# Whole float32 operands for the product of probabilities and values in the first of four batches

## The chip, the cores and the metric

The kernel runs on one core of a Trainium2 chip. The metric is the device time of one execution in microseconds (us). A core has five engines that work side by side, each through its own list of instructions in order: PE (TensorE, matrix products), DVE (VectorE), ACT (ScalarE), POOL (GpSimd) and SP (SyncE, which here only issues DMA transfers). PEld is PE's loading of the stationary operand, which can overlap a running product. An engine waits for another through semaphores.

## The reference

```python
def _attn_ref(q, k, v, tau):                       # q, k, v: (4, 8, 576, 64), float32
    scores = scale * np.matmul(q, k.transpose(0, 1, 3, 2))
    thresh = np.max(scores, axis=-1, keepdims=True) - tau
    scores = np.where(scores >= thresh, scores, -1000000000.0)
    scores = scores - np.max(scores, axis=-1, keepdims=True)
    attn = np.exp(scores)
    attn = attn / (np.sum(attn, axis=-1, keepdims=True) + 1e-09)
    return np.matmul(attn, v).astype(np.float32)
...
x = _moe_ref(x, w_in, w_out, alpha)    # h = x @ w_in (512 -> 2048); leaky max; @ w_out (2048 -> 512)
return _moe2_ref(x, w_in, w_out)       # h = x @ w_in; h * clip(h + 3, 0, 6) / 6; @ w_out
```

x has 2304 rows: 4 batches of 576 positions, 8 heads of 64 columns. The weights of both feed-forward networks (FFNs) come as float64 and are decoded to float32 on the chip.

## The kernel before

**Split operands.** Products run on operands of type float32r (`F32R`), which hold only the upper part of a float32. To keep the precision, a float32 operand is split: ACT copies it to float32r (`hi`), and another engine subtracts that from the source (`lo`). A product is then three: hi by hi, lo by hi, hi by lo.

**Attention.** The work goes through 16 pairs of heads (4 in each batch) and 9 tiles of 128 query rows in each pair, so a batch has 36 tiles. For tile `i` the stages are: `do_S` (scores, PE, into the PSUM tile `s`, of which there are 2), `soft_max` (DVE, maximum), `soft_exp` (ACT), `soft_keep` (DVE, threshold and sum), `soft_den` and `soft_rc` (POOL and DVE, reciprocal; POOL then scales the row `e`, L403, and copies its last 64 columns once more, L404), `do_T` (PE transposes four blocks of `e` as float32, L429), then the split of the transposed probabilities into `pt`, and once every two or three tiles a unit is complete: `do_R` transposes the last 64 columns (L448, split at L450 and L451), `do_PV` multiplies probabilities and values (PE, L465), and `do_x` adds the two halves of the result into `xo` (ACT L479, DVE L484). A pair has 4 units: two of 256 columns (buffer `ptu`) and two of 320 (buffer `ptw`).

**The product before.** The stationary operand `vn` is 128 wide: 64 columns of the upper parts of the values beside 64 of the lower ones. It meets 4 blocks of upper parts of the probabilities, one block in which the last 64 keys have upper over lower parts, and 4 blocks of lower parts, so a unit takes 9 products. The lower parts of the transposed probabilities come from DVE (L438), except that in the first two batches three tiles of nine (1, 4 and 7, `PE_LO`) take them from PE: a product with the negated identity `nidentr` (L435) subtracts the upper part in PSUM, and ACT copies the rest out (L436). The values are loaded by SP into a `raw` tile and split by ACT (L107) and POOL (L108; DVE for the first pair).

**FFNs.** From the end of the first batch on, the FFNs of batch b run in groups between the attention tiles of batch b + 1, after a fixed number of groups for each tile (`per`, with a lag of 3 tiles). Their first pass needs the decode of 64 weight chunks: ACT L136 and L137, DVE L138, L140 and L141, POOL L142, then a split. Six chunks are decoded early, during the first batch. The last batch's FFNs run alone at the end.

**Order.** The order of instructions on each engine is fixed when the program is built, by a scheduler that takes the code's order and priorities. At run time each engine keeps that order.

Of the kernel before, what the change touches and what calls it, by code (L numbers as in the profile page):

```python
# [9 lines left out]
F32 = mybir.dt.float32  # L10
F32R = mybir.dt.float32r
# [3 lines left out]
ALU = mybir.AluOpType  # L15
# [4 lines left out]
P = 128  # L20
NKT = 4
# The upper 32 bits of a float64, read as a float32: the least and greatest magnitude
# that float32's normal range holds.
# [9 lines left out]
def kernel(  # L33
# [13 lines left out]
    nc = tc.nc  # L47
    B, H, S, D = q.shape
# [4 lines left out]
    SM = 512  # L53
# [7 lines left out]
    # Weights decoded before the first FFN, and tiles by which the FFNs trail the attention.  # L61
    EARLY = 6
    LAG = 3
    # Tiles of a pair, up to tile PE_LO_END, whose lower parts come from the tensor engine.
    PE_LO = (1, 4, 7)
    PE_LO_END = 2 * PB
    # Chunks to a sum of the output.
# [4 lines left out]
    # Columns of a batch: 128 j + p holds position 4 p + j of the first 512; the other 64  # L72
    # positions of all batches make a block of their own.
# [22 lines left out]
    nidentr = const.tile([P, P], F32R, name="nidentr")  # L96
    nc.vector.tensor_single_scalar(nidentr, ident, -1.0, op=ALU.mult)
# [65 lines left out]
    # The FFNs in their order, each with the chunks of its weights; block None is the last  # L163
    # batch together with the last positions of all.
# [78 lines left out]
    # ------------------------------------------------------------------  # L243
    # attention, with the FFNs of the batches before it
    # ------------------------------------------------------------------
# [9 lines left out]
    # Queries of the two heads' last positions share a tile: each head's are beside zeros.  # L255
# [11 lines left out]
    # A pair of heads: of the first 512 positions, 4 to a partition, a block for each of the 4;  # L267
    # the last 64 of the one head are above those of the other, in block 4 between.
    def prep_load(pi, nm):
        if pi >= len(pairs):  # L270
            return
        b, hp = pairs[pi]
        src = {"q": q, "k": k, "v": v}[nm][b, 2 * hp:2 * hp + 2]
        t = a3.tile([P, 2, NB + 1, D], F32, tag="raw", name="raw")
        nc.sync.dma_start(t[:, :, 0:NB, :].rearrange("p h j d -> p h (j d)"),
                          src[:, 0:SM].rearrange("h (p j) d -> p h (j d)", j=NB))
        if nm == "v":
            for a in range(2):
                nc.sync.dma_start(t[64 * a:64 * a + 64, :, NB, :], src[:, SM:S].rearrange("h r d -> r h d"))
        else:  # L280
            for h in range(2):
                nc.sync.dma_start(t[64 * h:64 * h + 64, 0, NB, :], src[h, SM:S])
        st.setdefault(pi, {})["raw" + nm] = t.rearrange("p h j d -> p (h j) d")

    def prep_split(pi, nm):
        raw = st[pi].pop("raw" + nm)
        n = 2 * NB + 1
        if nm == "v":
            n += 1
            t = a2.tile([P, n, 2, D], F32R, tag="vn", name="vn")  # L290
        elif pi == 0 and nm == "q":
            t = a2.tile([P, 2 * NB + 2, 2, D], F32R, tag="vn", name="natq")
        else:
            t = a1.tile([P, n, 2, D], F32R, tag="nat", name="nat")
        raw = raw[:, 0:n]
        split(t[:, 0:n, 0, :], t[:, 0:n, 1, :], raw, nc.vector if pi == 0 else nc.gpsimd)
        st[pi]["nat" + nm] = t

    # Blocks 0 to 3 and 4 are the first head's columns; the second's begin with block 5, and
    # its last 64 come once more after block 8.  # L300
# [97 lines left out]
    # The last 64 probabilities of a row twice.  # L398
    def soft_rc(i):
        rc = small("rc", 3)  # L400
        nc.vector.reciprocal(rc, st.pop((i, "d")))  # L401
        e = st[i, "e"]
        nc.gpsimd.tensor_scalar(out=e[:, 0:S], in0=e[:, 0:S], scalar1=rc, scalar2=0.0, op0=ALU.mult, op1=ALU.add)  # L403
        nc.gpsimd.tensor_scalar(out=e[:, S:W], in0=e[:, SM:S], scalar1=1.0, scalar2=0.0, op0=ALU.mult, op1=ALU.add)  # L404

    # Where the transposed probabilities of a tile go: buffer, first column, and the unit
    # (head, first column, columns) that the tile completes.
# [8 lines left out]
    def pt_buf(i):  # L416
        nm = PLACE[i % NT][0]
        if i % NT in (0, 2, 7):
            ptb[nm] = a1.tile([P, 2 * NB + 1, {"u": 256, "w": 384}[nm]], F32R, tag="pt" + nm, name="pt" + nm,
                              bufs=2 if nm == "u" else 1)  # L420
        return ptb[nm]

    # Blocks 0 to 3: the upper parts of 128 keys each. Block 4: the upper parts of the last 64
    # over their lower parts. Blocks 5 to 8: the lower parts of 128 keys each.
    def do_T(i):
# [8 lines left out]
        if i < PE_LO_END and i % NT in PE_LO:  # L434
            nc.tensor.matmul(ps, lhsT=nidentr, rhs=pt[:, 0:NB], start=False, stop=True, skip_group_check=True)  # L435
            nc.scalar.copy(pt[:, NB + 1:], ps)  # L436
        else:
            nc.vector.tensor_tensor(out=pt[:, NB + 1:], in0=ps, in1=f32(pt[:, 0:NB]), op=ALU.subtract)  # L438

    def do_R(i):  # L440
# [5 lines left out]
        for j in range(m):  # L446
            e = st.pop((i - m + 1 + j, "e"))
            nc.tensor.transpose(ps[:, P * j:P * j + P], e[:, SM:W], ident)  # L448
        pt = ptb[nm][:, NB, c0 - (m - 1) * P:c0 + P]
        nc.scalar.copy(pt, ps)  # L450
        nc.vector.tensor_tensor(out=pt[64:P], in0=ps[64:P], in1=f32(pt[64:P]), op=ALU.subtract)  # L451

    def do_PV(i):
# [8 lines left out]
        pv = ps_ho.tile([P, SM], F32, tag="ho", name="pv")  # L462
        for kt in range(2 * NB + 1):
# [5 lines left out]
    def do_x(i):  # L469
# [8 lines left out]
        tl = a1.tile([P, 320], F32, tag="tl", name="tl")[hs]  # L478
        nc.scalar.copy(tl[:, 0:n], pv[ls, 0:n])  # L479
# [4 lines left out]
        nc.vector.tensor_tensor(out=xo[hs, d0:d0 + n], in0=pv[hs, 0:n], in1=tl[:, 0:n], op=ALU.add)  # L484
# [9 lines left out]
    # A group is 12 products of 512 columns: one chunk of 128 hidden features, or a quarter of  # L494
    # the output's sums over 4 chunks.
# [67 lines left out]
    # Rows of the output that a tile of 128 columns holds.  # L563
# [8 lines left out]
    # Weights that are decoded while there is no FFN yet.  # L572
# [18 lines left out]
    # No score reaches its row's maximum less a negative tau, and a row without any is  # L591
    # uniform: as if all scores were 0. So the scale of the queries is 0 then.
# [46 lines left out]
    # ------------------------------------------------------------------  # L639
    # both FFNs of the last batch together with the last positions  # L640
    # ------------------------------------------------------------------
# [84 lines left out]
```

## Time and profile before

| What | Value |
|---|---|
| Time, median of 3 runs (lowest to highest) | 1221.58 us (1220.2 to 1222.34) |
| Span of the profiled execution, first to last instruction | 1219.0 us |
| What lies around the span (median less span) | 2.6 us |
| PE, busy share of the span | 92% |
| DVE | 67% |
| POOL | 63% |
| ACT | 57% |
| Mean granted TensorE clock | 0.982 of full |

The profile is of one execution; its span lies 2.6 us under the median of the timed runs, and 1.2 us under the fastest. The shares are means over stages that differ much: the first 12 us are loads, up to 137 us only attention of the first batch and early decoding run, from 137 to 459 us FFNs of the first batch with all remaining decoding, then attention and FFNs without decoding, and from about 890 us FFNs alone. PE's busy time counts products whose ends are modelled, so it is above the time in which columns stream.

### The profile page before, as it was taken

The numbers are of one execution on the slowest core, as the hardware profiler recorded it, in microseconds if no ns is written. First come the engines' busy times: TensorE is split into PE (matmuls) and PEld (weight loads), VectorE is DVE, ScalarE is ACT, GpSimd is POOL, SyncE is SP. The second block draws the span as 40 slices with busy tenths as digits, with TensorE's granted clock in tenths as the row PEclk, the third lists the DMA queues.
The fourth block names the chain that finished last, engine by engine and source line by source line (L and its number), as shares of the span: only waits on it lengthen the run. The fifth ranks groups of instructions, "written<-read, shape, count | busy, mean of one in ns | idle before, by whom it ended". The sixth has DMA issues, their size and how long they took to land.

```text
span 1219.0 us, 18146 instructions
## 1 busy us (share of the span) xinstructions
PE 1124.4 (92%) x6008; PEld 949.6 (78%) x6008; DVE 814.9 (67%) x1607; ACT 699.7 (57%) x1280; POOL 770.5 (63%) x917
## 2 busy tenths in 40 slices
PE   5778988987788899999999999999999999999997
PEld 4667776875576688888888888887878888888886
DVE  7999997999899967687657576777645333332221
ACT  7888865766777765555665656455644222243432
POOL 4787798889779886766556776665533443434332
PEclk9889998999989999999999999999999999999999
DMA  6732345565557453424242444232224422222211
GB/s 196 227 115 74 97 142 170 157 184 167 184 154 219 141 163 105 120 80 113 77 121 79 131 137 121 70 96 74 71 78 129 118 60 68 61 61 63 67 35 52
DMA packets 95678, 139.51 MB, mean 114 GB/s; under 512 B 21472, under 2 KB 50656, under 8 KB 95584
## 3 DMA queue, kind: packets, MB, share of 16 engines
q1 hardware_dynamic: 95584, 138.36, 38.9%
q8 instruction: 47, 0.77, 0.3%
q14 instruction: 47, 0.39, 0.1%
HBM read 103.82 MB, written 25.17 MB: 106 GB/s over the span
## 4 chain that ended last, share of the span: by engine, by line
PE 56%; DVE 4%; issue 2%; POOL 2%; ACT 1%; DMA 1%; SPq 0%; POOLq 0%; DVEq 0%; ACTq 0%
PE h L204 24%; PE o L240 11%; PE o L234 9%; PE pv L465 3%; PE s L360 3%; PE t L429 2%; PE r L234 2%; PE r L240 2%; POOL wo L108 1%; DMA st<-wo 1%; PE pt L306 1%; DVE e L389 0%; PE r L448 0%; DVE wo L108 0%; DVE g L212 0%
## 5 line engine op out<-in xcount | busy, mean ns | idle before, releaser
L204 PE MATMUL h<-x,wi 128*128 128x512 f32 (+1 forms) x1536 | 360.2, 385 | 15.9 <-DVE g L212 4.8
L204 PEld LDWEIGHTS h<-x,wi 128*128 128x128 f32 x1536 | 275.0, 190 | 74.5 <-DVE g L212 5.5
L230 POOL TENSOR_TENSOR gs<-g,gs 128x512 fp32r<-128x512 f32 (+1 forms) x160 | 194.9, 1219 | 154.6 <-ACT gs L226 149.1
L240 PE MATMUL o<-wo,gs 128*128 128x512 f32 x768 | 195.8, 396 | 5.7 <-DVE g L220 1.8
L234 PE MATMUL o<-gs,wo 128*128 128x512 f32 x768 | 195.9, 397 | 1.3 <-POOL gs L230 0.8
L240 PEld LDWEIGHTS o<-wo,gs 128*128 128x128 f32 x768 | 141.0, 188 | 36.4 <-DVE g L220 2.9
L234 PEld LDWEIGHTS o<-gs,wo 128*128 128x128 f32 x768 | 141.2, 189 | 29.6 <-POOL gs L230 1.0
L226 ACT CAST gs<-g 128x512 fp32r<-128x512 f32 (+1 forms) x160 | 92.9, 580 | 87.3 <-DVE g L212 46.2
L220 DVE SCALAR_TENSOR_TENSOR g<-m,h 128x512 f32<-128x512 f32 x80 | 50.5, 631 | 132.4 <-ACT m L218 131.9
L403 POOL TENSOR_SCALAR e<-e,rc 128x576 f32<-128x576 f32 x144 | 115.1, 804 | 20.0 <-DVE rc L401 13.9
L389 DVE SCALAR_TENSOR_TENSOR e<-s,thr,e 128x576 f32<-128x576 f32 x144 | 116.0, 813 | 9.4 <-ACT e L382 7.5
L372 DVE TENSOR_REDUCE nmx<-s 128x1 f32<-128x576 f32 x144 | 107.1, 748 | 17.0 <-PE s L360 15.5
L382 ACT ACTIVATE e<-s,nmx 128x576 f32<-128x576 f32 x144 | 106.4, 748 | 19.4 <-DVE nmx L372 11.2
L209 DVE TENSOR_SCALAR m<-h,alpha_sb 128x512 f32<-128x512 f32 x80 | 55.3, 692 | 91.9 <-PE h L204 91.9
L360 PE MATMUL s<-ka,qt 128*128 128x288 f32 x512 | 103.5, 324 | 12.7 <-DVE e L389 11.5
L107 ACT CAST wo<-st 128x512 fp32r<-128x512 f32 x99 | 59.2, 620 | 91.4 <-DMA st<-wo 81.7
L218 ACT ACTIVATE m<-h,three 128x512 f32<-128x512 f32 x80 | 51.6, 646 | 102.9 <-PE h L204 102.6
L108 POOL TENSOR_TENSOR wo<-st,wo 128x512 fp32r<-128x512 f32 x58 | 76.0, 1324 | 51.8 <-ACT wo L107 51.8
L108 POOL TENSOR_TENSOR wi<-st,wi 128x512 fp32r<-128x512 f32 x58 | 74.8, 1291 | 45.7 <-ACT wi L107 44.9
L107 ACT CAST wi<-st 128x512 fp32r<-128x512 f32 x99 | 61.2, 619 | 66.2 <-PE h L204 27.9
L429 PE MATMUL t<-ident,e 128*128 128x128 f32 x576 | 91.4, 283 | 7.9 <-ACT ptu L436 3.0
L142 POOL TENSOR_TENSOR f<-f,low 128x512 uint32<-128x512 uint32 x64 | 86.3, 1348 | 19.5 <-issue 4.0
(103 smaller groups left out, 1942.7 us busy)
## 6 DMA issues: line engine op xcount, KB each, us to landing
st<-wi SPq DMA_DIRECT2D x99, 256.0 KB, 2.6
st<-wo SPq DMA_DIRECT2D x99, 256.0 KB, 2.6
raw<-in_moe_w_in_dram SPq DMA_DIRECT2D x32, 512.0 KB, 4.1
raw<-in_moe_w_out_dram SPq DMA_DIRECT2D x32, 512.0 KB, 3.9
ka<-ka SPq DMA_DIRECT2D x30, 304.0 KB, 4.2
wi<-f SPq DMA_DIRECT2D x32, 256.0 KB, 3.1
wo<-f SPq DMA_DIRECT2D x32, 256.0 KB, 4.1
raw<-in_k_dram SPq DMA_DIRECT2D x16, 256.0 KB, 2.9
```

The source lines that it names most:

```text
L107: nc.scalar.copy(hi, src)
L108: lo_eng.tensor_tensor(out=lo, in0=src, in1=f32(hi), op=ALU.subtract)
L204: nc.tensor.matmul(h[:, :n], lhsT=w[:, ws, kt * P:(kt + 1) * P], rhs=x[:, xs, kt, :n], start=(i == 0), stop=(i == len(steps) - 1))
L230: nc.gpsimd.tensor_tensor(out=gs[:, 1, :n], in0=g[:, :n], in1=f32(gs[:, 0, :n]), op=ALU.subtract)
L234: nc.tensor.matmul(o[:, :n], lhsT=w[:, ws, dt * P:(dt + 1) * P], rhs=gs[:, gsel, :n], start=fresh and start and i == 0, stop=stop and i == ...
L240: nc.tensor.matmul(o[:m, :], lhsT=gs[:, gsel, tt * P:tt * P + m], rhs=w[:, ws, :], start=start and i == 0, stop=stop and i == 2)
L360: nc.tensor.matmul(ps[:, half, 0:SH], lhsT=w, rhs=s["k"][:, a, h * W + half * SH:h * W + half * SH + SH], start=(n == 0), stop=(n == len(m ...
L372: nc.vector.tensor_reduce(out=nmx, in_=st[i, "s"][:, :, 0:SH], axis=AX.XY, op=ALU.max, negate=True)
L382: nc.scalar.activation(v2(e[:, 0:S]), st[i, "s"][:, :, 0:SH], AF.Exp, bias=st.pop((i, "nmx")), scale=1.0)
L389: nc.vector.scalar_tensor_tensor(out=v2(e), in0=st.pop((i, "s"))[:, :, 0:SH], scalar=st.pop((i, "thr")), in1=v2(e), op0=ALU.is_ge, op1=ALU ...
L403: nc.gpsimd.tensor_scalar(out=e[:, 0:S], in0=e[:, 0:S], scalar1=rc, scalar2=0.0, op0=ALU.mult, op1=ALU.add)
L429: nc.tensor.matmul(ps[:, j], lhsT=e[:, P * j:P * j + P], rhs=ident, is_transpose=True, start=(j == 0), stop=True, skip_group_check=True)
```

## The change

In batch 0 (`WHOLE = 1`) nothing of the product is split. The values are loaded straight into a tile of the pool and tag that the split values had (`a2`, tag `vn`, two buffers), and stay float32. The transposed probabilities are copied once from PSUM, as float32; the lower parts (L438) and the subtraction at L451 go, and so do the copy of the last 64 columns (L404) and the split of the values. A unit takes 5 products with both operands float32, and its result has 64 rows instead of 128, so `do_x` copies it once with ACT instead of copying one half and adding the other.

The route over the negated identity (`PE_LO`) is taken out altogether. In batch 0 nothing replaces it; in batch 1, where 12 tiles had used it, those tiles' lower parts now come from DVE, as in the later batches.

```diff
-    # Tiles of a pair, up to tile PE_LO_END, whose lower parts come from the tensor engine.
-    PE_LO = (1, 4, 7)
-    PE_LO_END = 2 * PB
+    WHOLE = 1
...
-    nidentr = const.tile([P, P], F32R, name="nidentr")
-    nc.vector.tensor_single_scalar(nidentr, ident, -1.0, op=ALU.mult)
...
     def prep_load(pi, nm):
...
+        whole = nm == "v" and b < WHOLE
+        if whole:
+            t = a2.tile([P, 2, 2, NB + 1, D], F32, tag="vn", name="vw")[:, 0]
+        else:
+            t = a3.tile([P, 2, NB + 1, D], F32, tag="raw", name="raw")
...
     def prep_split(pi, nm):
         raw = st[pi].pop("raw" + nm)
+        if nm == "v" and pairs[pi][0] < WHOLE:
+            st[pi]["natv"] = raw
+            return
...
     def soft_rc(i):
...
-        nc.gpsimd.tensor_scalar(out=e[:, S:W], in0=e[:, SM:S], scalar1=1.0, scalar2=0.0, op0=ALU.mult, op1=ALU.add)
+        if i >= WHOLE * PB:
+            nc.gpsimd.tensor_scalar(out=e[:, S:W], in0=e[:, SM:S], scalar1=1.0, scalar2=0.0, op0=ALU.mult, op1=ALU.add)
...
     def do_T(i):
...
         nc.scalar.copy(pt[:, 0:NB], ps)
-        if i < PE_LO_END and i % NT in PE_LO:
-            nc.tensor.matmul(ps, lhsT=nidentr, rhs=pt[:, 0:NB], start=False, stop=True, skip_group_check=True)
-            nc.scalar.copy(pt[:, NB + 1:], ps)
-        else:
+        if i >= WHOLE * PB:
             nc.vector.tensor_tensor(out=pt[:, NB + 1:], in0=ps, in1=f32(pt[:, 0:NB]), op=ALU.subtract)
...
     def do_R(i):
...
-            nc.tensor.transpose(ps[:, P * j:P * j + P], e[:, SM:W], ident)
+            if i < WHOLE * PB:
+                nc.tensor.transpose(ps[0:64, P * j:P * j + P], e[:, SM:S], ident)
+            else:
+                nc.tensor.transpose(ps[:, P * j:P * j + P], e[:, SM:W], ident)
         pt = ptb[nm][:, NB, c0 - (m - 1) * P:c0 + P]
+        if i < WHOLE * PB:
+            nc.scalar.copy(pt[0:64], ps[0:64])
+            return
...
     def do_PV(i):
...
+        if b < WHOLE:
+            for kt in range(NB + 1):
+                r = P if kt < NB else 64
+                nc.tensor.matmul(pv[0:64, 0:n], lhsT=vn[0:r, (NB + 1) * h + kt], rhs=src[0:r, kt, c0:c0 + n],
+                                 start=(kt == 0), stop=(kt == NB))
+            st[i, "v"] = pv
+            return
...
     def do_x(i):
...
+        if b < WHOLE:
+            nc.scalar.copy(xo[hs, d0:d0 + n], pv[0:64, 0:n])
+        else:
+            tl = a1.tile([P, 320], F32, tag="tl", name="tl")[hs]
+            nc.scalar.copy(tl[:, 0:n], pv[ls, 0:n])
+            nc.vector.tensor_tensor(out=xo[hs, d0:d0 + n], in0=pv[hs, 0:n], in1=tl[:, 0:n], op=ALU.add)
```

The scheduler places the instructions anew. PE's list before, at the third to fifth tile of the first pair, that is the unit of buffer `ptw` (`s` are scores, `t` and `r` transposes, `pt` the preparation of the next pair, `pv` the product):

```order
L448 MATMUL r<-ident,e 128x128 x3
L435 MATMUL t<-ptw,nidentr 128x512
L465 MATMUL pv<-ptw,vn 128x320 x4
L306 MATMUL pt<-identr,nat 128x128 x3
L360 MATMUL s<-ka,qt 128x288 x4
L429 MATMUL t<-ident,e 128x128 x4
L360 MATMUL s<-ka,qt 128x288 x4
L306 MATMUL pt<-identr,nat 128x128 x3
L465 MATMUL pv<-ptw,vn 128x320 x5
```

The same unit in the changed program, whose lines 366, 437, 454, 312 and 477 are the lines 360, 429, 448, 306 and 465 of before:

```order
L454 MATMUL r<-ident,e 64x128 x3
L312 MATMUL pt<-identr,nat 128x128 x3
L477 MATMUL pv<-ptw,vw 64x320 x5
L437 MATMUL t<-ident,e 128x128 x4
L366 MATMUL s<-ka,qt 128x288 x4
```

The nine products, which stood in two pieces with scores and transposes between them, have become five that stand together, and the product with `nidentr` is gone.

DVE's list before, in the second batch beside the first FFN groups, from the fourth tile of its first pair to the end of its `ptw` unit (`ptw<-t` is a lower part, L438; `m` and `g` belong to the FFN, `low` and `f` to the decoding):

```order
L438 TENSOR_TENSOR ptw<-t,ptw 128x4x128
L377 TENSOR_SCALAR thr<-nmx,ntau_sb 128x1
L389 SCALAR_TENSOR_TENSOR e,sm<-s,thr,e 128x576
L140 TENSOR_SCALAR f<-f 128x512
L209 TENSOR_SCALAR m<-h,alpha_sb 128x512
L141 TENSOR_SCALAR f<-f 128x512
L372 TENSOR_REDUCE nmx<-s 128x1
L212 SCALAR_TENSOR_TENSOR g<-h,m 128x512
L389 SCALAR_TENSOR_TENSOR e,sm<-s,thr,e 128x576
L401 RECIPROCAL rc<-den 128x1
L377 TENSOR_SCALAR thr<-nmx,ntau_sb 128x1
L451 TENSOR_TENSOR ptw<-r,ptw 64x384
```

The same place in the changed program (L443 is the lower part, L462 the subtraction of L451):

```order
L443 TENSOR_TENSOR ptw<-t,ptw 128x4x128
L383 TENSOR_SCALAR thr<-nmx,ntau_sb 128x1
L378 TENSOR_REDUCE nmx<-s 128x1
L443 TENSOR_TENSOR ptw<-t,ptw 128x4x128
L137 TENSOR_SCALAR f<-f 128x512
L135 TENSOR_SCALAR low<-raw_2166 128x512
L383 TENSOR_SCALAR thr<-nmx,ntau_sb 128x1
L407 RECIPROCAL rc<-den 128x1
L138 TENSOR_SCALAR f<-f 128x512
L395 SCALAR_TENSOR_TENSOR e,sm<-s,thr,e 128x576 x2
L206 TENSOR_SCALAR m<-h,alpha_sb 128x512
L462 TENSOR_TENSOR ptw<-r,ptw 64x384
```

A second lower part has come in, that of the fifth tile, which PE and ACT made before. In both programs 10 decodes stand ahead of the first FFN activation on DVE, and all 64 ahead of the 17th.

## Rows read from the trace of the kernel before

**Rows 1.** Busy time of each engine by stage; x counts instructions; PEclk is granted clock.

```profile
core 0: us, PE busy (x) PEld busy (x) DVE busy (x) ACT busy (x) POOL busy (x), PEclk, DMA share, GB/s
0.00:12.00 12.00, 4.95 (x26) 4.33 (x27) 4.34 (x14) 6.92 (x13) 0.70 (x6) 1.00 0.47 105
12.00:80.00 68.00, 48.48 (x268) 42.09 (x267) 63.50 (x153) 55.66 (x102) 54.24 (x80) 0.85 0.70 214
80.00:137.00 57.00, 48.93 (x342) 42.03 (x343) 53.76 (x140) 49.08 (x95) 38.59 (x78) 1.00 0.25 67
137.00:459.00 322.00, 275.92 (x1413) 225.69 (x1412) 287.37 (x522) 226.31 (x404) 278.83 (x299) 0.97 0.55 167
459.00:1219.00 760.00, 746.10 (x3965) 635.41 (x3963) 405.97 (x782) 361.70 (x669) 398.13 (x457) 1.00 0.31 87
```

**Rows 2.** PE's timeline about the first FFN product: start, length, line, count.

```profile
136.98 0.64 PE L465 MATMUL pv<-ptu,vn 128*128 128x256 f32 x4
137.46 2.66 PE L204 MATMUL h<-x,wi 128*128 128x512 f32 x11
```

**Rows 3.** DVE's groups of instructions, 12 to 137 us: busy, mean ns, idle before.

```profile
L389 DVE SCALAR_TENSOR_TENSOR e<-s,thr,e 128x576 f32<-128x576 f32 x40 | 32.2, 812 | 3.0 <-ACT e L382 2.3
...
L438 DVE TENSOR_TENSOR ptw<-t,ptw 128x512 fp32r<-128x512 f32 x16 | 10.7, 676 | 0.7 <-PE pv L465 0.7
L138 DVE TENSOR_SCALAR low<-raw 128x512 uint16<-128x512 uint16 x12 | 8.8, 735 | 0.2
...
L484 DVE TENSOR_TENSOR xo<-pv,tl 64x256 f32<-64x256 f32 (+1 forms) x16 | 7.2, 450 | 0.8 <-ACT tl L479 0.5
...
L451 DVE TENSOR_TENSOR ptw<-r,ptw 64x384 fp32r<-64x384 f32 (+1 forms) x8 | 4.0, 494 | 0.2
L451 DVE TENSOR_TENSOR ptu<-r,ptu 64x256 fp32r<-64x256 f32 x8 | 3.4, 428 | 0.2
...
L108 DVE TENSOR_TENSOR vn<-raw,vn 128x640 fp32r<-128x640 f32 x1 | 0.8, 826 | 2.0 <-ACT vn L107 2.0
```

**Rows 4.** ACT's and POOL's groups that the change touches, 12 to 137 us.

```profile
L436 ACT CAST ptu<-t 128x512 fp32r<-128x512 f32 x8 | 4.7, 585 | 0.0
L107 ACT CAST vn<-raw 128x640 fp32r<-128x640 f32 x5 | 3.6, 727 | 0.6 <-DMA raw<-in_v_dram 0.5
...
L436 ACT CAST ptw<-t 128x512 fp32r<-128x512 f32 x4 | 2.4, 598 | 0.0
L404 POOL TENSOR_SCALAR e<-e 128x64 f32<-128x64 f32 x38 | 10.6, 285 | 1.0
L108 POOL TENSOR_TENSOR vn<-raw,vn 128x640 fp32r<-128x640 f32 x5 | 7.8, 1552 | 0.0
```

**Rows 5.** PE's timeline, 100 to 110 us, all at full granted clock.

```profile
100.56 0.90 PE L465 MATMUL pv<-ptw,vn 128*128 128x320 f32 x5
101.29 0.60 PE L429 MATMUL t<-ident,e 128*128 128x128 f32 x4
101.65 0.77 PE L360 MATMUL s<-ka,qt 128*128 128x288 f32 x4
102.25 0.38 PE L306 MATMUL pt<-identr,nat 128*128 128x128 f32 x3
102.47 0.40 PE L448 MATMUL r<-ident,e 128*128 128x128 f32 x2
102.79 0.82 PE L465 MATMUL pv<-ptw,vn 128*128 128x320 f32 x4
...
105.55 0.63 PE L429 MATMUL t<-ident,e 128*128 128x128 f32 x4
105.94 0.99 PE L465 MATMUL pv<-ptw,vn 128*128 128x320 f32 x5
106.76 0.39 PE L435 MATMUL t<-ptu,nidentr 128*128 128x512 f32 x1
106.99 0.69 PE L360 MATMUL s<-ka,qt 128*128 128x288 f32 x4
107.52 0.63 PE L465 MATMUL pv<-ptu,vn 128*128 128x256 f32 x4
107.99 0.38 PE L448 MATMUL r<-ident,e 128*128 128x128 f32 x2
```

**Rows 6.** PEld's timeline, same place: weight loads of float32 transposes.

```profile
101.15 0.50 PEld L429 LDWEIGHTS t<-ident,e 128*128 128x128 f32 x4
101.62 0.56 PEld L360 LDWEIGHTS s<-ka,qt 128*128 128x128 f32 x4
```

**Rows 7.** DVE's groups, 137 to 459 us.

```profile
L138 DVE TENSOR_SCALAR low<-raw 128x512 uint16<-128x512 uint16 x52 | 47.6, 916 | 0.2
...
L438 DVE TENSOR_TENSOR ptw<-t,ptw 128x512 fp32r<-128x512 f32 x19 | 12.8, 680 | 4.9 <-ACT ptw L433 4.9
```

**Rows 8.** DVE's group L138, 80 to 130 us, one decode.

```profile
L138 DVE TENSOR_SCALAR low<-raw 128x512 uint16<-128x512 uint16 x1 | 0.5, 460 | 0.0
```

**Rows 9.** PE's timeline: the last use of the buffer `natq`.

```profile
11.51 0.54 PE L306 MATMUL pt<-identr,natq 128*128 128x128 f32 x3
```

**Rows 10.** SP's timeline of DMA issues: second pair's values, first weight chunk.

```profile
12.66 0.37 SPq L275 DMA_DIRECT2D raw<-in_v_dram  x1
...
16.20 0.59 SPq L130 DMA_DIRECT2D raw<-in_moe_w_in_dram  x1
```

More of the change, by code (lines that the diff above doesn't have):

```diff
@@ L273, in prep_load @@
         src = {"q": q, "k": k, "v": v}[nm][b, 2 * hp:2 * hp + 2]
-        t = a3.tile([P, 2, NB + 1, D], F32, tag="raw", name="raw")
+        whole = nm == "v" and b < WHOLE
[3 more added lines that the diff above has]
+            t = a3.tile([P, 2, NB + 1, D], F32, tag="raw", name="raw")
         nc.sync.dma_start(t[:, :, 0:NB, :].rearrange("p h j d -> p h (j d)"),
                           src[:, 0:SM].rearrange("h (p j) d -> p h (j d)", j=NB))
-        if nm == "v":
+        if whole:
+            nc.sync.dma_start(t[0:64, :, NB, :], src[:, SM:S].rearrange("h r d -> r h d"))
+        elif nm == "v":
             for a in range(2):
@@ L418, in pt_buf @@
         if i % NT in (0, 2, 7):
-            ptb[nm] = a1.tile([P, 2 * NB + 1, {"u": 256, "w": 384}[nm]], F32R, tag="pt" + nm, name="pt" + nm,
-                              bufs=2 if nm == "u" else 1)
+            ptb[nm] = a1.tile([P, 2 * NB + 1, {"u": 256, "w": 384}[nm]], F32 if i < WHOLE * PB else F32R, tag="pt" + nm,
+                              name="pt" + nm, bufs=2 if nm == "u" else 1)
         return ptb[nm]
@@ L477, in do_x @@
         hs, ls = slice(64 * h, 64 * h + 64), slice(64 - 64 * h, 128 - 64 * h)
-        tl = a1.tile([P, 320], F32, tag="tl", name="tl")[hs]
-        nc.scalar.copy(tl[:, 0:n], pv[ls, 0:n])
         if "xo" not in st[pi]:
@@ L483, in do_x @@
         d0 = 0 if nm == "u" else 256
-        nc.vector.tensor_tensor(out=xo[hs, d0:d0 + n], in0=pv[hs, 0:n], in1=tl[:, 0:n], op=ALU.add)
+        if b < WHOLE:
[4 more added lines that the diff above has]
+            nc.vector.tensor_tensor(out=xo[hs, d0:d0 + n], in0=pv[hs, 0:n], in1=tl[:, 0:n], op=ALU.add)
         if t == NT - 1:
```

## The prediction

> **What bounds the kernel now.** I read the busy times by stage first [rows 1], since the change touches only the first two batches. From 12 to 137 us, where batch 0's attention runs, DVE is busy 63.50 + 53.76 = 117.3 of 125 us, 94%. ACT has 104.7 (84%), POOL 92.8 (74%). PE's 97.4 counts modelled ends, so I work out its streaming below. DVE bounds this stage, and the stage ends where PE starts the first FFN product at 137.46 us [rows 2]. From 137 to 459 us DVE is busy 287.37 of 322 us (89%) and POOL 278.83 (87%), because all remaining decodes run there. After 459 us PE is busy 746 of 760 us: whatever is won or lost before is carried to the end, since PE has next to no idle time in which it could disappear.
>
> **What leaves DVE in batch 0.** Of 36 tiles, 24 have their lower part on DVE: 24 x 0.68 = 16.3 us. The 16 units lose the subtraction of L451 (8 x 0.494 + 8 x 0.428 = 7.4) and the addition of L484 (16 x 0.450 = 7.2), and the first pair's split of values goes (0.8) [rows 3]. Together 31.7 us, and DVE would be left with 117.3 - 31.7 = 85.6 of the 125.
>
> **What leaves ACT and POOL.** ACT loses 12 copies L436 (7.1 us) and 4 casts of values (2.9): 104.7 - 10.0 = 94.7. Its other copies stay with the same columns; that they keep their time as float32 copies I take from `do_x`, whose one copy has the form of the old L479. POOL loses 36 copies of 0.285 (10.3) and 3 splits of 1.552 (4.7): 92.8 - 15.0 = 77.8 [rows 4].
>
> **What PE gets.** From the starts in PE's timeline [rows 5] I take the time for which one product holds PE, the distance to the next group's start over the count. The product of 320 columns: (101.29 - 100.56) / 5 = 0.146 us; of 256: (107.99 - 107.52) / 4 = 0.118. Scores: 0.60 / 4 and 0.53 / 4, mean 0.142. A float32 transpose of 128 columns: 0.39 / 4 = 0.098. The last columns' transpose: 0.16; a preparation transpose: 0.073; the product with `nidentr`: 0.23. A pair has 40 score products (5.7 us), 36 transposes (3.5), 9 (1.4) and 19 (1.4) of the other two kinds, 3 products with `nidentr` (0.7) and 18 + 18 products with values (4.75). Before, that is 17.4 us for a pair.
>
> The change removes 0.7 + 4.75 and adds 10 + 10 products of whole float32 operands, which the trace doesn't show. From below: the float32 transpose, 0.098 / 128 = 0.77 ns a column, gives 0.245 and 0.196 us, 4.4 us for a pair. From above: a whole float32 is two of the kernel's float32r parts, so the product is four part products; at 0.146 and 0.118 each that makes 10 x 0.584 + 10 x 0.472 = 10.6 us, if each of the four hides its weight load as now. If none does, each adds the load of a float32 transpose, (101.62 - 101.15) / 4 = 0.118 us [rows 6], and the pair has 20.0 us. I take 10.6: a transpose only moves values through, while the kernel itself already needs three of the four part products for less precision. PE then has 12.0 + 10.6 = 22.6 us for a pair, 90 for the batch.
>
> The Trainium skill ("FP8 and Floating Point Precision", TensorE Precision Notes) says that a true float32 product makes four passes through the array. No run here shows that yet; by it the sum would be the same 10.6, and the bounds above stand without it.
>
> **Which engine is next.** The stage 12 to 137 us holds 40 threshold steps [rows 3], so 4 tiles of batch 1 as well, whose scores and transposes cost PE some 1.2 us each: 95 us in all. That is at full clock. The granted clock in this stage is 0.85 for 68 us and 1.00 for 57 [rows 1], mean 0.918, and I keep it: 95 / 0.918 = 103.5 us. PE would be the busiest engine of the stage, ACT (94.7) close behind, DVE at 85.6. How full the busiest can be, two stages show: 94% where the next engine is at 84%, and 89% where the next stands at 87% [rows 1]. The second is the likeness here: 103.5 / 0.89 = 116 us. The stage would be 125 - 116 = 9 us shorter. So of 31.7 us taken from DVE about 9 arrive.
>
> **What batch 1 pays.** 12 tiles get back a lower part on DVE, 12 x 0.68 = 8.2 us [rows 7], while PE and ACT lose 12 products and 12 copies there. DVE is 89% busy in that stage, so 8.2 is the upper bound and 0 the lower. For the lower one speaks that much of DVE's busy time is no work: a decode step L138 takes 0.916 us on average there [rows 7], but 0.460 alone [rows 8], while the lower part keeps to 0.68. So the bound is DVE and POOL in each other's way more than DVE's own sum, and DVE still idles 35 of 322 us. I take 2 us.
>
> The Trainium skill ("SBUF — State Buffer", Who interferes with whom) says why: DVE and POOL share a port pair as an exclusive lock, which the one-input SBUF steps of a decode can take, while a DVE instruction with at most one SBUF input outside those modes doesn't contend. The steady 0.68 beside the doubled L138 agrees. Strictly by this rule the 12 subtractions would cost POOL nothing, the term would be 0 and the time 2 us lower than I say.
>
> **Loads.** The values of the second pair now go into the buffer of `natq`, whose last transposes start at 11.51 us [rows 9]; the load was issued at 12.66, with the first weight chunk behind it on SP at 16.20 [rows 10], so it waits for nothing new. The third pair's values wait until the first pair's last product; they are used nine tiles later, some 27 us at the present pace of 125 us for 40 tiles. I cost both at nothing; the cover gone, the weight chunks on SP behind them would be late by the same time.
>
> **The sum.** -9 + 2 = -7 us on the profiled span of 1219.0, so 1212. The span lies 2.6 us under the median of the timed runs, and I carry the difference: 1221.6 - 7 = 1214.6, rounded to 1215. A difference of 0.2% (2.4 us) is about what the measurement can tell.
>
> **Rivals.**
>
> *PE becomes a worse bound than DVE was (slower).* The place is the stage 12 to 137 us; the mechanism is PE's list, in which a unit's five products now stand together before the next transposes and scores: 5 x 0.584 = 2.9 us in one piece where four products of 0.146 stood. It decides from the point at which the 9 - 2 us are used up: PE at 123 x 0.89 x 0.918 = 100.5 us, less the 5 of the other tiles 95.5, a pair 23.9, so products of 11.9 us instead of 10.6, 13% dearer. At five part products' time (13.2 for a pair) PE has 105.8, the stage 129.5, and with 4 us in batch 1 the time is 1221.6 + 8.5 = 1230. With all weight loads bare (20.0) PE has 133 us; at full clock and 94% that is 141, and with 8.2 the time is 1246. For it: PE is the engine whose cost the trace doesn't show. Against: PE streams now only about 75 of these 125 us. Chance 0.28.
>
> *The gain is eaten (no change).* Stalls that don't come from DVE stay, PE and ACT at 95 and 104 us keep the stage at 121 to 124, and batch 1 costs 2 to 4: 1219 to 1224. For it: DVE waits little now, so the engines' orders fit each other, and these orders are new. Chance 0.13.
>
> *The products are cheap.* At the transpose's rate PE has 71 us, 77 at the present clock; ACT leads with 94.7, and at 94% the stage takes 101: -24, and with nothing lost in batch 1 the time is 1197. Partly so, 1197 to 1207. Against: it asks for half the part products. Chance 0.11.
>
> *My forecast*, 1207 to 1219, has 0.48.
>
> **How the numbers follow.** The time is that of the forecast, 1215. Faster by over 0.2% holds the forecast and the cheap case: 0.59. Within 0.2%: 0.13. Slower: 0.28. The range leaves out the cheap case's lower half and the slower rival's upper half: 1203 to 1231. Since cases of both signs hold chance, the forecast's own range is 1207 to 1219.
>
> **What the new profile would show.** First FFN product on PE near 128 us instead of 137.46; DVE busy about 86 us up to there and PE the fullest engine, with products that hold it 0.47 and 0.58 us. If a product holds PE longer, or DVE's scores wait for PE behind them, the first term fails. From the first FFN product to the end of decoding the stage should be 322 us plus about 2; if it is 330, the second fails. If the granted clock in the first half rises from 0.85 to 1.00, the gain is larger, 125 - 95 / 0.89 = 18 us.

## The result, and the profile after

The changed kernel takes 1235.89 us (median of 4 runs, 1233.28 to 1237.51), the kernel before beside it 1221.96 us (4 runs, 1220.2 to 1223.91). The ratio is 1.0109, interval 1.0089 to 1.013: slower by 13.9 us. The prediction said 1215 in a range of 1203 to 1231, so it was wrong in sign, and the time lies outside its range. The profiled execution took 1237.51 us, its span is 1235.7.

The busy times by stage of the changed kernel, with the stage ends moved to where they now lie (columns as in [rows 1]):

```profile
core 0: us, PE busy (x) PEld busy (x) DVE busy (x) ACT busy (x) POOL busy (x), PEclk, DMA share, GB/s
12.00:80.00 68.00, 55.95 (x281) 36.25 (x280) 56.04 (x134) 52.91 (x97) 48.01 (x62) 0.92 0.71 216
80.00:142.00 62.00, 57.38 (x332) 38.35 (x331) 37.53 (x103) 42.62 (x84) 32.01 (x56) 1.00 0.21 56
142.00:473.00 331.00, 276.98 (x1403) 226.13 (x1402) 296.61 (x536) 220.49 (x391) 273.82 (x296) 0.95 0.53 162
473.00:1235.00 762.00, 747.45 (x3967) 635.35 (x3965) 406.12 (x780) 361.79 (x669) 398.77 (x458) 1.00 0.30 87
```

Batch 0's attention now lasts to 142 us instead of 137, as PE's timeline at the first FFN product shows (L201 is L204 of before):

```profile
141.61 0.74 PE L483 MATMUL pv<-ptu,vn 128*128 128x256 f32 x4 [0.46 <-ACT ptu L441]
142.19 1.09 PE L201 MATMUL h<-x,wi 128*128 128x512 f32 x4
```

So the stage that should have become 9 us shorter became 4.7 longer (142.19 - 137.46), the next is 331 us instead of 322, and the last has grown by 2. Most of what the change promised for DVE did come: its busy time from 12 us to the stage's end fell from 117.3 us to 56.04 + 37.53 = 93.6, 23.7 us of the 31.7 that the prediction took off. But DVE now waits. Its group of maxima, 12 to 142 us, which need the scores from PE, has 24.3 us of idle time ahead of it:

```profile
L395 DVE SCALAR_TENSOR_TENSOR e<-s,thr,e 128x576 f32<-128x576 f32 x40 | 32.4, 813 | 7.2 <-ACT e L388 6.7
L378 DVE TENSOR_REDUCE nmx<-s 128x1 f32<-128x576 f32 x41 | 30.7, 753 | 24.3 <-PE s L366 24.2
```

In the kernel before the same group, 12 to 137 us, had 1.9 us:

```profile
L372 DVE TENSOR_REDUCE nmx<-s 128x1 f32<-128x576 f32 x41 | 30.6, 749 | 1.9 <-PE s L360 1.3
```

The chart of waits of the changed kernel from 80 to 142 us (total, times, longest) says the same of the later half:

```profile
DVE nmx L378 <- PE s L366: 16.6, 16, 2.3
POOL den L401 <- DVE e L395: 5.1, 6, 2.0
ACT xo L501 <- PE pv L477: 4.3, 3, 2.1
```

The bound went from DVE at 94% to PE, which is 57.38 / 62 = 93% busy from 80 to 142 us while DVE is at 61%. PE's timeline from 74.6 us on (start, length, line, count of records):

```profile
74.59 0.60 PE L437 MATMUL t<-ident,e 128*128 128x128 f32 x4
74.95 0.78 PE L366 MATMUL s<-ka,qt 128*128 128x288 f32 x4
75.57 0.37 PE L312 MATMUL pt<-identr,nat 128*128 128x128 f32 x3
75.78 0.38 PE L454 MATMUL r<-ident,e 128*64 128x128 f32 x2
76.02 0.63 PE L437 MATMUL t<-ident,e 128*128 128x128 f32 x4
76.58 2.37 PE L477 MATMUL pv<-ptw,vw 128*64 128x320 f32 x8
78.88 0.80 PE L366 MATMUL s<-ka,qt 128*128 128x288 f32 x4
79.52 0.60 PE L437 MATMUL t<-ident,e 128*128 128x128 f32 x4
80.04 0.75 PE L477 MATMUL pv<-ptw,vw 64*64 64x320 f32 x2
80.72 0.41 PE L454 MATMUL r<-ident,e 128*64 128x128 f32 x2
...
82.02 1.94 PE L477 MATMUL pv<-ptu,vw 128*64 128x256 f32 x8
83.90 0.44 PE L312 MATMUL pt<-identr,nat 128*128 128x128 f32 x3
```

Each product of whole operands leaves two records, so "x8" is four products. They hold PE 2.30 / 4 = 0.575 us at 320 columns and 1.88 / 4 = 0.47 at 256. The prediction had 0.584 and 0.472: the price of the new operation was right. The five products of a unit don't stand together here, as they do in the unit whose list is shown above: four do, and the fifth, over the last 64 keys, follows scores and transposes (80.04 us) and holds PE 0.68 us.

### The profile page after: what moved, and what is told of

Its sections match the earlier page's. It is cut to its first block, busy times and chain, and to the rows that moved or that the text cites. A ratio compares the mean times of both kernels' runs of the same rounds, so it can differ in the third digit from the quotient of the medians.

```text
span 1235.7 us, 18011 instructions
## 1 busy us (share of the span) xinstructions
PE 1142.7 (92%) x6000; PEld 940.4 (76%) x6000; DVE 800.3 (65%) x1561; ACT 684.4 (55%) x1252; POOL 753.8 (61%) x878
## 4 chain that ended last, share of the span: by engine, by line
PE 52%; DVE 7%; issue 4%; POOL 4%; ACT 2%; DMA 2%; SPq 0%; POOLq 0%; DVEq 0%; ACTq 0%
PE h L201 22%; PE o L237 11%; PE o L231 8%; PE pv L483 3%; PE s L366 2%; PE r L231 2%; PE r L237 2%; PE t L437 2%; POOL wo L105 2%; DMA st<-wo 1%; DVE f L137 1%; DVE e L395 1%; POOL nat L105 1%; DVE g L217 1%; DVE low L135 1%
## 5 line engine op out<-in xcount | busy, mean ns | idle before, releaser
L201 PE MATMUL h<-x,wi 128*128 128x512 f32 (+1 forms) x1536 | 363.9, 387 | 21.2 <-DVE acc L561 6.8
L201 PEld LDWEIGHTS h<-x,wi 128*128 128x128 f32 x1536 | 276.2, 191 | 80.4 <-DVE g L209 6.8
L366 PE MATMUL s<-ka,qt 128*128 128x288 f32 x512 | 99.7, 317 | 12.0 <-DVE e L395 11.1
L401 POOL TENSOR_SCALAR den<-sm 128x1 f32<-128x1 f32 x144 | 32.1, 223 | 113.8 <-DVE e L395 76.8
L366 PEld LDWEIGHTS s<-ka,qt 128*128 128x128 f32 x512 | 77.8, 195 | 25.5 <-DVE e L395 12.4
```

What stands on the lines that cost most here:

```text
L201: nc.tensor.matmul(h[:, :n], lhsT=w[:, ws, kt * P:(kt + 1) * P], rhs=x[:, xs, kt, :n], start=(i == 0), stop=(i == len(steps) - 1))
L366: nc.tensor.matmul(ps[:, half, 0:SH], lhsT=w, rhs=s["k"][:, a, h * W + half * SH:h * W + half * SH + SH], start=(n == 0), stop=(n == len(m ...
```

## The experiments

Three numbers carry the comparison: the time, the start of the first FFN product on PE (the end of the first stage, 137.5 us before), and the length of the stage from there to the 33rd group of FFN first products, at which all decoding is done. In the expectations of before_nolo1 and whole_pelo1 this group is called the 49th by mistake; the figures given there are those of the 33rd. The last column is the median time less the first FFN product, so what batch 1 and all later work takes; it joins timed runs with one profile and is good to a few us. How far the first FFN product moves by itself is seen in kernels whose batch 0 is alike: 137.5 and 137.7 us (before, before_nolo1), and 142.2, 143.0 and 142.9 (after, whole_pelo1, order_alone). Beside the other kernels the one before had medians of 1222.5 to 1223.1.

| Kernel | Median us (runs) | Ratio to before, interval | First FFN product | To 33rd group | Time less first FFN product |
|---|---|---|---|---|---|
| before (beside single, four, before_nolo1, whole_pelo1) | 1223.32 (15) | | 137.5 | 321.4 | 1085.8 |
| after | 1235.89 (4) | 1.0109, 1.0089 to 1.013 | 142.2 | 331.1 | 1093.7 |
| single | 1215.17 (4) | 0.9933, 0.9915 to 0.9951 | 124.4 | 326.6 | 1090.8 |
| two | 1220.34 (1) | | 130.2 | 324.6 | 1090.1 |
| three | 1223.0 (1) | | 139.7 | 320.5 | 1083.3 |
| four | 1225.45 (10) | 1.0014, 1.0002 to 1.0026 | 142.2 | 319.7 | 1083.3 |
| whole_dve | 1235.39 (4) | 1.0112, 1.0095 to 1.0129 | 141.8 | 326.2 | 1093.6 |
| before_nolo1 | 1227.73 (6) | 1.0033, 1.0021 to 1.0046 | 137.7 | 325.6 | 1090.0 |
| whole_pelo1 | 1229.87 (4) | 1.0045, 1.0028 to 1.0061 | 143.0 | 324.4 | 1086.9 |
| order_alone | 1235.82 (4) | 1.0104, 1.0075 to 1.0134 | 142.9 | 325.2 | 1092.9 |
| whole_copy | 1233.64 (6) | 1.0095, 1.0063 to 1.0128 | 142.9 | 322.3 | 1090.7 |
| pair2 | 1228.04 (7) | 1.0048, 1.003 to 1.0065 | 142.4 | 320.9 | 1085.6 |
| pairs13 | 1230.02 (6) | 1.0057, 1.0041 to 1.0072 | 140.9 | 325.1 | 1089.1 |
| pairs01 | 1229.18 (6) | 1.005, 1.0033 to 1.0066 | 142.5 | 326.5 | 1086.7 |

**One to four passes (single, two, three, four).** Theory: PE's time for the products sets the first stage. Rival: something else of the change does (order, buffers, the lost route over PE). In these kernels batch 0's product runs on the upper parts alone, once to four times over, so the lower parts are left out and the sum is taken several times; the rest is as in the changed kernel, but for the values, which ACT copies to float32r.

```diff
+    REP = 1        # 1, 2, 3 or 4
...
-                nc.tensor.matmul(pv[0:64, 0:n], lhsT=vn[0:r, (NB + 1) * h + kt], rhs=src[0:r, kt, c0:c0 + n],
-                                 start=(kt == 0), stop=(kt == NB))
+                for u in range(REP):
+                    nc.tensor.matmul(pv[0:64, 0:n], lhsT=vn[0:r, (NB + 1) * h + kt], rhs=src[0:r, kt, c0:c0 + n],
+                                     start=(kt == 0 and u == 0), stop=(kt == NB and u == REP - 1))
```

One pass: 

> The changed kernel with the same 5 products per unit in batch 0, but on upper parts alone (probabilities and values cast to float32r by ACT, lower parts left out of the computation), so that a product is one pass instead of the two records of 0.25 to 0.29 us that a whole float32 product took. PE time theory (PE's four-part products are what holds batch 0): 80 x (0.54 - 0.13) = 33 us leave PE, ACT becomes the fullest, the first FFN product stands near 118 to 124 us instead of 142, and the total falls to 1211 to 1218. Order theory (pieces, new order and loads hold batch 0, not the products' price): the first FFN product stays at 137 to 142 and the total at 1231 or more.

Four passes: 

> As the run before, but each of the 5 products is issued four times in a row (the result of batch 0 is four times too large): the streaming of a whole float32 product, 4 x 0.118 and 4 x 0.146 us, out of ordinary one-pass products. PE time theory: as the changed kernel, first FFN product at 140 to 145 us, total 1232 to 1240. If whole float32 products cost more than their streaming (weight loads or changes of array shape that nothing hides), this is faster than the changed kernel: first FFN product at 135 or below.

Two passes: 

> Each product of batch 0 issued twice on upper parts (two passes; lower parts left out, result of batch 0 twice too large). With one pass the first FFN product stood at 124.4 us, with four at 142.2. If PE is the bound only from some number of passes on, two passes stay near the first: 124 to 128 us. If every pass costs alike, it stands at 130.

Three passes: 

> Each product of batch 0 issued three times on upper parts (lower parts left out, result three times too large). PE time theory: one pass more on the 80 products is 80 x 0.13 = 10.6 us of PE, so with PE as the bound the first FFN product stands about 8 to 10 us before that of four passes, 132 to 134 us; if every pass costs alike, 136.

The first FFN product comes at 124.4, 130.2, 139.7 and 142.2 us. With one pass, everything that the change takes off DVE, ACT and POOL is worth 137.5 - 124.4 = 13.1 us; passes two to four take back 5.8, 9.5 and 2.5, together 17.8. (Two and three passes ran once each; three passes came later than both expectations, and four took 1225.45 us where 1232 to 1240 were expected, of which more below.) The changed kernel, with float32 operands, stands at 142.2, where four passes stand. So what the products cost PE is enough to explain the loss of the first stage, and no other part of the change is needed for it. In the kernel of four passes 18 of the 20 products of one unit hold PE from 100.93 to 103.87, 2.94 us, 0.163 each:

```profile
100.93 3.01 PE L481 MATMUL pv<-ptw,vw 128*64 128x320 f32 x18
103.87 0.79 PE L369 MATMUL s<-ka,qt 128*128 128x288 f32 x4
```

The passes don't arrive in equal parts: each adds 10.6 us of PE's time, the stage takes 56% of it. The granted TensorE clock differs between these kernels, which no run held fixed: with one to four passes it was 0.85, 0.85, 0.82 and 0.90 from 12 to 80 us, and 1.00, 0.97, 0.97 and 1.00 from there to the first FFN product. Multiplied by it, the stages from 12 us on are 102, 106, 114 and 123 us (an estimate, as if the whole stage went with that clock), so the passes add 4, 8 and 9 of the 10.6 us each. In the same measure the kernel before has 115 and the changed one 125.

**DVE's work put back (whole_dve).** The changed kernel, with the 24 lower parts that DVE made in batch 0 made again, and not used.

```diff
-        if i >= WHOLE * PB:
+        if i < WHOLE * PB:
+            if i % NT not in (1, 4, 7):
+                nc.vector.tensor_tensor(out=pt[:, NB + 1:], in0=ps, in1=pt[:, 0:NB], op=ALU.subtract)
+        else:
             nc.vector.tensor_tensor(out=pt[:, NB + 1:], in0=ps, in1=f32(pt[:, 0:NB]), op=ALU.subtract)
```

> The changed kernel with the 24 lower parts of batch 0 computed by DVE again, into blocks that nothing reads: 16.3 us of DVE are put back, PE keeps its whole float32 products. PE time theory: DVE was idle beside PE in batch 0, so the first FFN product stays at 142 to 145 us and the total within 3 us of the changed kernel. Rival, that DVE still decides part of batch 0 (the first half, where decoding runs): the first FFN product moves to 148 to 155 us.

```profile
12.00:80.00 68.00, 55.81 (x276) 36.12 (x276) 60.84 (x144) 52.98 (x97) 46.84 (x62) 0.92 0.70 215
80.00:142.00 62.00, 58.38 (x342) 39.72 (x343) 46.47 (x120) 43.66 (x85) 32.69 (x58) 1.00 0.22 56
```

The stage rows show the added work in DVE's column (60.84 and 46.47 us where the changed kernel has 56.04 and 37.53), and nothing is lost by it: the first FFN product comes at 141.8, the time is that of the changed kernel. The engine that was the bound now has room for these 16 of the 32 us that were taken off. This is the second half of the proof: more work on PE moves the end, this work on DVE doesn't. As nothing reads the blocks, the run doesn't show what a product that waits for them would cost.

**Batch 1's lower parts (before_nolo1, whole_pelo1).** The kernel before with the twelve lower parts of batch 1 on DVE, and the changed kernel with them on PE again.

```diff
-    PE_LO_END = 2 * PB
+    PE_LO_END = PB
```

> The kernel before with nothing changed but that the second batch's 12 lower parts come from DVE. Theory that DVE pays for them: batch 0 as before (first FFN product at 137 us), the stretch behind it 7 to 10 us longer than 321, total 1228 to 1232. Rival: no change, 1221 to 1224. My prediction's term was 2 us, 1224.

```diff
-        if i >= WHOLE * PB:
+        if WHOLE * PB <= i < 2 * PB and i % NT in (1, 4, 7):
+            nc.tensor.matmul(ps, lhsT=nidentr, rhs=pt[:, 0:NB], start=False, stop=True, skip_group_check=True)
+            nc.scalar.copy(pt[:, NB + 1:], ps)
+        elif i >= WHOLE * PB:
```

> The changed kernel with the second batch's 12 lower parts put back on PE and ACT (product with the negated identity). Theory that DVE pays for them: the stretch from the first FFN product to the 49th group of FFN first products shrinks from 331 us by 7 to 10 us to 321 to 324, total 1226 to 1229. Rival, that the stretch is longer because batch 0 ends later or in another order: it stays at 329 to 333 and the total at 1235.

Alone, this part of the change costs 1227.73 - 1223.32 = 4.4 us (by the interval 2.6 to 5.6); put back into the changed kernel, the ratio falls from 1.0109 to 1.0045, 7.8 us (about 5 to 11 by the two intervals). Both are more than the 2 of the prediction. The stretch to the 33rd group is 4.2 us longer in the first and 6.7 shorter in the second, both short of the theory's 7 to 10. The subtractions themselves stayed as they were, in the stage from 138 to 463 us of the first of these kernels:

```profile
L438 DVE TENSOR_TENSOR ptw<-t,ptw 128x512 fp32r<-128x512 f32 x23 | 15.5, 679 | 3.4 <-ACT ptw L433 3.3
```

**Order and load (order_alone, whole_copy).** The changed kernel and that of four passes reach the first FFN product at the same time, and yet their times differ by 10 us, all of it behind that point. Two kernels look for it: one with the changed kernel's own instructions in another order from batch 1 on (in the trace 324 of PE's 6000 instructions and 297 of DVE's 1561 stand where the changed kernel has one of another line or tile), one with the values loaded and copied as in the kernel of four passes, but as float32.

```diff
-        with tc.high_priority(offset=50):
+        with tc.high_priority(offset=50 if i < PB else 60):
```

> The changed kernel with the scheduler's priority of the later attention stages raised from the second batch on (60 instead of 50): the same instructions, batch 0 in the same order, another order behind. Theory that the stretch from the first FFN product to the 33rd group of FFN first products (331.1 us in the changed kernel, 319.7 with four passes, same work) depends on the order: it moves by several us to anywhere between 318 and 336. Rival, that the 12 lower parts on DVE fix it: 329 to 333.

```diff
-        whole = nm == "v" and b < WHOLE
+        whole = False
...
-            st[pi]["natv"] = raw
+            t = a2.tile([P, 2, 2, NB + 1, D], F32, tag="vn", name="vw")[:, 0].rearrange("p h j d -> p (h j) d")
+            nc.scalar.copy(t, raw)
+            st[pi]["natv"] = t
```

> The changed kernel, with the values of batch 0 loaded into a raw tile and copied as float32 by ACT, as in the kernel with four one-pass products, in place of the load straight into the tile that the product reads. Theory (the 10 us between the changed kernel and the one with four one-pass products come from the order of instructions in the second stage or from the load, not from the products): the first FFN product near 142 us. If the load is the cause, the stretch from it to the 33rd group of FFN first products is about 320 us and the time about 1225; if only the order is, it lies anywhere from 320 to 331 us and the time from 1225 to 1236. Rival (the float32 products themselves cost more in the time of the second stage): 331 us and 1236, and nothing else.

Neither gains: 1235.82 and 1233.64, both intervals overlap that of the changed kernel. In the profiled executions the stage to the 33rd group spans 325.2 and 322.3 us where it was 331.1, without the medians following. So I read the 331 as the upper end of a scatter between executions and orders, not as a cost with a place of its own. The load is not the cause of the 10 us, and another order didn't bring them either; what sets the kernels of three and four passes (both 1083.3 behind the first FFN product) apart from the seven others with batch 1's lower parts on DVE (1090.0 to 1093.7) stays open. The granted clock alone isn't it: its mean is 0.978 in the kernel of three passes, 0.983 in that of four and 0.982 in the changed one.

**Whole operands in some pairs only (pair2, pairs13, pairs01).** Theory: the stage goes by whichever engine is fuller, so some pairs with whole operands even DVE and PE out. Rival: every such pair costs PE's time. Batch 1 and all other pairs are as before.

```diff
-    WHOLE = 1
+    WH = (2,)      # (1, 3), (0, 1)
...
-        if b < WHOLE:
+        if pi in WH:
```

> Whole float32 products only in the third pair of batch 0; everywhere else the split product, with the lower parts from PE on three tiles of nine as in the kernel before, in batch 1 too. Theory (batch 0 goes by whichever of DVE and PE is fuller, and before both are near full: DVE 94% and PE about 86% of the last 57 us): a quarter of the exchange evens them out, DVE loses about 8 us and PE gains about 5, the first FFN product comes 2 to 4 us earlier than in the kernel before, batch 1 costs nothing, and the time is 1218 to 1221. Rival (PE was already the bound before, so that each added pass costs its time): the first FFN product comes 1 to 3 us later and the time is 1223 to 1226.

> Whole float32 products in the second and fourth pair of batch 0 alone, the rest as in the kernel before, batch 1 too. Theory: DVE loses 16 us and PE gains 10, PE is then the fuller of the two; the first FFN product stays within 2 us of that of the kernel before and the time is 1220 to 1224. Rival (PE alone bounds, half of the full change's effect): 2 to 3 us later, 1224 to 1226. If instead the later stage of the full change was slow because of whole products in batch 0 and not because of the lower parts of batch 1, the stretch from the first FFN product to the 33rd group of FFN first products would lie above the 321 us of before here.

> Whole float32 products in the first and second pair of batch 0 alone, the rest as in the kernel before, batch 1 too. In the kernel before PE is busy 71% from 12 to 80 us, where these two pairs run, and 86% from 80 to 137. Theory (the products cost time only where PE has no room, so the loss of about 4 us seen with the third pair alone and with the fourth lies in the later stretch): the 19th tile's maximum at 74 to 76 us as before, the first FFN product at 136.5 to 138.5, the time 1221 to 1225. Rival (any pair with whole products costs 3 to 5 us, wherever it stands): the first FFN product at 140.5 to 142.5 and the time 1226 to 1230.

The theory fell, three times. The third pair alone delays the first FFN product by 4.9 us, the second and fourth by 3.4, the first and second by 5.0, all four by 4.7. In the first two kernels the rival expected less than that (up to 3 us, 1224 to 1226); in the last one its figures came out. So none of these choices gains, whether PE had been busy 71% there or 86%.

That every pair costs the same doesn't follow, since the clock differs here too. From 12 to 80 us it was 0.85 before, 0.92 with all four pairs whole, and in these kernels, in their order above:

```profile
12.00:80.00 68.00, 49.03 (x266) 42.74 (x265) 64.28 (x151) 55.57 (x101) 53.56 (x81) 0.82 0.70 218
12.00:80.00 68.00, 53.22 (x271) 42.28 (x271) 61.17 (x145) 54.25 (x101) 51.67 (x72) 0.80 0.72 216
12.00:80.00 68.00, 52.76 (x256) 34.26 (x255) 53.13 (x125) 48.21 (x90) 46.66 (x60) 0.90 0.69 212
```

Behind 80 us it is 1.00 in all of them. In the measure of above the stage is 118, 115 and 124 us long, where it is 115 before and 125 with all four: 3 us more, none, 8 and 10. By this estimate the nearly equal delays hide unequal work. The place of the delay differs as well. With all four pairs whole the maxima of the 19th and 28th tile start at 74.8 and 100.6 us, as before (74.7, 100.8), and the whole loss arises behind them; with the first two pairs alone the 19th already comes at 78.7. What set the clock in each is not shown.

The kernel with the third pair whole shows why averages mislead; its rows from 75 us on:

```profile
75.00:90.00 15.00, 10.64 (x78) 9.64 (x79) 14.28 (x36) 10.66 (x21) 8.17 (x16) 1.00 0.13 39
90.00:105.00 15.00, 13.14 (x81) 9.02 (x80) 8.35 (x23) 10.68 (x20) 9.02 (x14) 1.00 0.34 84
105.00:120.00 15.00, 14.16 (x87) 9.95 (x85) 9.96 (x29) 11.82 (x23) 9.39 (x18) 1.00 0.16 43
120.00:135.00 15.00, 12.80 (x88) 10.65 (x86) 14.07 (x37) 12.65 (x25) 10.18 (x21) 1.00 0.34 85
```

While split pairs run, DVE is 95% and 94% busy and PE has idle time; while the whole pair's products run, PE is at 88 and 94% and DVE at 56 and 66%. I read this so that the engines don't run far enough ahead of each other to lend one pair's idle time to the next, and that every pair goes at the pace of its own fuller engine; no run tested the distance by itself. Why four such pairs cost no more than one is not settled, and the clock is one part of it that no run separates; the delay of the third pair arises at its products (the 32nd tile's maximum at 116.4 us instead of 112.1) and stays.

The pairs also serve as a control for batch 1: with its lower parts on PE (before, whole_pelo1, and these three) the last column holds 1085.6 to 1089.1.

## Why the prediction was wrong

**The step that failed is PE's sum and how full it can be**: "95 / 0.918 = 103.5 us", "103.5 / 0.89 = 116 us", and so "of 31.7 us taken from DVE about 9 arrive". The right engine was named as the next bound and the new products were priced right, but the rest of PE's time was put too low. From 74.58 to 91.23 us PE works without any wait at full granted clock:

```profile
74.58:91.23 16.65, 16.65 (x99) 11.09 (x97) 12.10 (x31) 12.31 (x24) 9.18 (x15) 1.00 0.24 78
```

By the prediction's prices its contents (28 transposes at 0.098, 24 scores at 0.142, 9 preparations at 0.073, 6 of the last columns at 0.16, 5 products at 0.584 and 10 at 0.472) are 15.4 us. The stretch took 16.65, 8% more. The prices were the distances of neighbours in [rows 5] where instructions follow one another fastest. Of the 1.2 us more, 0.8 lie at the float32 transposes: four of them take 0.36 us here where scores follow (74.59 to 74.95), but 0.52 to 0.59 in the five places where a whole product does (two are in the timeline above: 76.02 to 76.58, 79.52 to 80.04). The prediction had thrown away PE's busy time because its ends are modelled, and said "PE streams now only about 75 of these 125 us". The page's 97.4 of [rows 1] was nearer the truth: 20.6 us more on top of it (10.6 - 0.7 - 4.75, four times) is 118 of 125 us, which would have named PE as a bound about as tight as DVE was; divided by the prediction's 0.89 it gives 133 us.

If the whole stage is like that stretch (an estimate), PE's sum is 95 x 1.08 = 102.6. With it in place of 95 the prediction's own formula gives 102.6 / 0.918 / 0.89 = 125.6 us, no gain. The granted clock rose, as it held possible, from 0.85 to 0.92 in the first part, mean 0.958 over the stage; that gives 120.3. The stage took 130.2, so PE was full to 102.6 / 0.958 / 130.2 = 82%, not 89%. By this estimate the term is mis-sized twice, by 10 us each, and the clock gave 5 back.

DVE's term was off as well, without deciding anything: 85.6 us were forecast and 93.6 measured. The prediction subtracted mean lengths, and DVE's instructions overlap (in [rows 1] it is busy 117.3 us, while the lengths of its groups in that stage add up to 133); the decode step L138, L135 of the changed kernel, also grew from 735 to 829 ns.

**"Batch 1: I take 2 us"** measured 4.4 in the order of before, up to 7.8 in that of after, within its bounds of 0 to 8.2. The row of a doubled L138 [rows 7, 8] had been read as a sign that DVE's sum doesn't set the pace; adding 12 x 0.68 = 8.2 us to it moved the end by half of that or more. By the Trainium skill ("SBUF — State Buffer", Who interferes with whom) these subtractions don't contend with POOL. The trace agrees in that they keep 679 ns; the inference that they cost nothing was wrong, since the same twelve instructions on a DVE that is 89% busy made the kernel 4.4 us longer.

**The sum.** 4.7 us in batch 0 and 4.4 to 7.8 in batch 1 make 9.1 to 12.5 of the 13.9. The other 1.4 to 4.8 are of the size by which these kernels' remainders scatter, and no part of the change was shown to cause them.

**The rivals.** "PE becomes a worse bound than DVE was" came true, with 142.2 us for its 141.5 (129.5 + 12), but not for its reason: it asked for products 13% dearer (12 by its own sum, 11.9 to 10.6), and they were not; even with the fifth product at 0.68 us a unit of 320 columns is 2.98 us to the forecast 2.92. Of its one piece of five products the timeline shows four together (DVE's longest waits for scores are 2.3 us, about their length), but no run changed the piece without its passes, so its share isn't shown. "The products are cheap" is out: a float32 product is not at a transpose's rate. The Trainium skill's four passes for a true float32 product ("FP8 and Floating Point Precision", TensorE Precision Notes) agree with 0.575 and 0.47 us against 4 x 0.146 and 4 x 0.118 [rows 5], and with the first FFN product at 142.2 in both kernels.

**What was costed at nothing.** The load straight into the tile: 142.9 and 1233.6 us with a raw tile and a copy, no difference that can be measured.

## What to carry to other kernels

When work is moved to an engine, take the busy share that the profile gives it as the upper bound and the nearest distances of its instructions as the lower one, and forecast a gain only if it survives the upper one; here the two gave 116 and 133 us, on both sides of the 130 measured. An engine at 78% on average that gets work for another 17% of the stage can be a new bound, and giving it the work in some parts only didn't help. Relieving the engine that bounds (worth 13 us here) pays only as far as the next one lets it, and one kernel with the new work cut to a quarter shows both numbers at once.

## What the runs showed of the hardware

- A product with both operands float32 stands in the trace as two records and holds PE about as long as four float32r products: 0.575 us at 320 columns, 0.47 at 256, where one float32r product takes 0.146 and 0.118 in the kernel before (with a stationary operand twice as wide), and 0.148 and 0.117 with the same shape in the kernel of three passes (12 in 1.77 us from 104.18 us, 12 in 1.40 from 108.00).
- A PE without a wait and at full granted clock took 16.65 us for work that is 15.4 by the shortest distances between instructions of the same kind.
- The granted clock from 12 to 80 us, a mean over stretches at full and at half clock, was 0.85 with one pass (PE busy 48.36 of the 68 us), 0.90 with four (55.53) and 0.92 with whole operands (55.95). With three passes it was 0.82 at 53.47 busy, and with whole operands in the second and fourth pair alone 0.80 at 53.22, so busy time alone doesn't order it. Kernels whose batch 0 is alike had the same clock there: 0.85 in before and before_nolo1, 0.92 in after, whole_pelo1 and order_alone.
